# A residual add taken from VectorE and given to an accumulating transfer on GpSimd's queue

## The chip, the cores and the metric

The kernel runs on one core of one Trainium2 chip. The metric is the device time of one execution in microseconds (us). Five engines work in the core, each with its own queue of instructions taken in order: TensorE (PE in the profile, with its weight loads as PEld), VectorE (DVE), ScalarE (ACT), GpSimd (POOL) and SyncE (SP), which here only issues transfers. Engines and transfers wait for each other through semaphores.

## The reference

One block of a network over x of shape (1, 2048, 512), in float32. Two halves follow each other, each normalised, scaled and shifted, and each added to x through a gate (ga, gb) that comes from a small product of `silu(c)` with `w_mod`:

```python
h = _layernorm(x) * (1 + ca) + sa
x = x + ga * irfft2(rfft2(h) * (w_r + 1j * w_i))      # spectral half
h = _layernorm(x) * (1 + cb) + sb
act = mish(h @ w1 + b1)                               # 512 -> 1376
x = x + gb * (act @ w2)                               # 1376 -> 512
```

The change concerns only the last line: x plus gb times the output of the second product.

## The kernel before

x stays in the core as `x`, 128 partitions by 16 rows by 512 floats (`x[:, n, :]` for row group n). The first 170 us or so compute the spectral half; nothing in it is touched here.

The second half works on eight blocks b = 0 to 7 of 256 rows (two row groups each, n = 2b and 2b+1). The 1376 hidden features are cut into six tiles, so that there are `total = 48` steps s, six for each block; the queues are filled in the order in which the code is written (a manual schedule). A call `mlp(s)` does, in this order:

- `up(s)`: TensorE multiplies by w1 (L796, L798) into PSUM banks tagged A and D, two buffers each.
- `front(s)`: ScalarE adds the bias (L806) and VectorE adds a second PSUM half (L807); this frees the banks.
- `halves(s-1)`: ScalarE casts the activation to `ah` (L758), VectorE takes the rest as `al` (L759). TensorE uses each value as such a pair.
- `back(s)`: ScalarE's Mish (L813), and for most steps four small VectorE sums (L823).
- `down(s-2)`: TensorE multiplies by w2 (L849) into four banks of the block.

A block's sum is ready in the second step of the next block (i = 1). There `gather(b)` copies two banks out on ScalarE (L872, L873), and `chain(b)` adds them on VectorE (L878 to L886) into `rows`, which is `modr[:, 0:2]`, 128 x 1024 floats, one buffer for all blocks. One step later (i = 2) `residual(b)` finishes the sum (L891, L893), multiplies `rows` by the gate (L894), adds `rows` to the two row groups of `x` (L896), and SyncE stores these to the output (L898, 512 KB).

The last block differs. Its feature tiles come in another order, its step order is written so that most of its sum is gathered early: `gather(7)` and `chain(7)` stand in step 45, and `residual(7)` in step 46. Block 6 has its `chain` in step 43 and its `residual` in step 44, so `chain(7)`, which writes `rows` again, follows `residual(6)` by one step, where for the earlier blocks five steps lie between. For the rest of block 7 the gate is multiplied into w2 ahead of time (`gate_w2`, L778 on GpSimd, after loads by SyncE at L747), the plain tiles are split into pairs (`plain_w2`, L758 and L759), and `finish` runs the last products (`last_down`, L862 and L865) and adds them to `x` from PSUM (L938), with three small stores (L939).

Of the kernel before, what the change touches and what calls it, by code (L numbers as in the profile page):

```python
# [10 lines left out]
ALU = mybir.AluOpType  # L11
# [9 lines left out]
NB = 8  # L21
# [11 lines left out]
def tile_spectral_block(ctx: ExitStack, tc: tile.TileContext, x_d, w1_d, b1_d, w2_d,  # L33
                        c_d, xt_d, wm_d, wq_d, wz_d, kr_d, km_d, kc_d, ki_d, kf_d, kv_d, kw_d, kp_d, out_d):
    nc = tc.nc
# [831 lines left out]
    rows = modr[:, 0:2]  # L867
# [21 lines left out]
    def residual(b):  # L889
        p, q = done.pop(b)  # L890
        nc.vector.tensor_tensor(rows[:, 1, 256:], rows[:, 1, 256:], q[:, 0:256], op=ALU.add)  # L891
        if b < NB - 1:
            nc.vector.tensor_tensor(rows[:, 0, 256:], rows[:, 0, 256:], p[:, 256:], op=ALU.add)  # L893
        nc.vector.tensor_tensor(rows, rows, gbr.unsqueeze(1).to_broadcast([P, 2, D]), op=ALU.mult)  # L894
        xb = x[:, 2 * b:2 * b + 2, :]
        nc.vector.tensor_tensor(xb, xb, rows, op=ALU.add)  # L896
        if b < NB - 1:
            nc.sync.dma_start(ov[:, 2 * b:2 * b + 2, :], xb)  # L898

# [3 lines left out]
    def mlp(s, parts):  # L903
        b, i = divmod(s, NT)
        nxt = 2 * b + 2 if b < NB - 1 else None
        up(s)
        if i == 4 and nxt:
            for g in range(2):
                transpose_in(nxt, g)
        front(s)  # L910
        halves(s - 1, parts)
        parts = back(s)
        if i == 3 and nxt:
            norm_pair(nxt)
        if i == 4 and nxt:
            for g in range(2):
                split_in(nxt, g)
        down(s - LAG)
        if i == 1 and b:
            gather(b - 1)  # L920
            chain(b - 1)
        if i == 2 and b:
            residual(b - 1)
        if s == total - 3:
            gather(b)
            chain(b)
        if s == total - 2:
            residual(b)
        return parts
# [237 lines left out]
```

## Time and profile before

| What | Value |
|---|---|
| Median of 3 runs | 381.94 us (381.69 to 382.84) |
| Profiled execution, first to last instruction (span) | 380.1 us |
| Median less that span | 1.84 us |
| TensorE busy | 373.7 us (98%) |
| VectorE busy | 300.2 us (79%) |
| ScalarE busy | 250.5 us (66%) |
| GpSimd busy | 99.1 us (26%) |
| Granted TensorE clock | 1.000 |

For the profiled execution no time is given but its span; what lies around the span is taken as the 1.84 us between it and the median of the runs.

In the profile, L896 is line 896 of the kernel. A row of the timeline gives the start in us from the beginning of the span, the time in us that the merged instructions take together, engine, line, operation, what is written and read, the count, and in brackets how long the engine had been idle and what ended that. A row of a source line gives the smallest, median and largest duration in ns. The chain of waits is followed back from the last instruction of the kernel.

### The profile page before, as it was taken

The numbers are of one execution on the slowest core, as the hardware profiler recorded it, in microseconds if no ns is written. First come the engines' busy times: TensorE is split into PE (matmuls) and PEld (weight loads), VectorE is DVE, ScalarE is ACT, GpSimd is POOL, SyncE is SP. The second block draws the span as 40 slices with busy tenths as digits, with TensorE's granted clock in tenths as the row PEclk, the third lists the DMA queues.
The fourth block names the chain that finished last, engine by engine and source line by source line (L and its number), as shares of the span: only waits on it lengthen the run. The fifth ranks groups of instructions, "written<-read, shape, count | busy, mean of one in ns | idle before, by whom it ended". The sixth has DMA issues, their size and how long they took to land.

```text
span 380.1 us, 7142 instructions
## 1 busy us (share of the span) xinstructions
PE 373.7 (98%) x2612; PEld 340.0 (89%) x2612; DVE 300.2 (79%) x688; ACT 250.5 (66%) x532; POOL 99.1 (26%) x134
## 2 busy tenths in 40 slices
PE   8999999998999999999999999999999999999996
PEld 8999967778999989998998998998998999899985
DVE  2898968886989989989749758757865976887994
ACT  1798789995497558865844845845765674685751
POOL 0588747883664611300000000000000010017000
PEclk9999999999999999999999999999999999999999
DMA  7999997776454221111000100100100200222011
GB/s 235 380 354 344 362 359 237 252 231 212 128 140 143 77 85 58 56 30 55 3 0 2 55 2 0 58 0 3 55 2 0 78 0 2 75 67 82 2 55 55
DMA packets 21746, 41.14 MB, mean 108 GB/s; under 512 B 4016, under 2 KB 7184, under 8 KB 21456
## 3 DMA queue, kind: packets, MB, share of 16 engines
q1 hardware_dynamic: 19552, 33.75, 26.3%
q10 hardware_dynamic: 2160, 6.95, 6.2%
q8 instruction: 20, 0.33, 0.3%
q14 instruction: 14, 0.11, 0.1%
HBM read 36.49 MB, written 4.20 MB: 107 GB/s over the span
## 4 chain that ended last, share of the span: by engine, by line
PE 93%; DVE 3%; ACT 1%; DMA 1%; issue 0%; SPq 0%; ACTq 0%
PE bank L849 24%; PE bank L796 21%; PE bank L798 10%; PE bank L707 4%; PE bank L717 4%; PE bank L708 4%; PE bank L498 4%; PE bank L208 4%; PE bank L547 3%; PE bank L253 3%; PE bank L841 2%; PE bank L862 2%; PE bank L478 2%; PE bank L686 2%; PE bank L255 1%; PE bank L254 1%
## 5 line engine op out<-in xcount | busy, mean ns | idle before, releaser
L806 ACT ACTIVATE buf<-bank,b1n 128x256 f32<-128x256 f32 (+1 forms) x88 | 40.8, 471 | 66.8 <-PE bank L798 64.2
L807 DVE TENSOR_TENSOR buf<-buf,bank 128x256 f32<-128x256 f32 (+1 forms) x88 | 35.4, 417 | 37.3 <-ACT buf L806 37.2
L759 DVE TENSOR_TENSOR al<-buf,ah 128x512 fp32r<-128x512 f32 (+2 forms) x85 | 52.9, 645 | 0.9 <-ACT ah L758 0.9
L778 POOL TENSOR_TENSOR buf<-buf,modr 128x512 f32<-128x512 f32 (+1 forms) x3 | 4.0, 1322 | 182.8 <-DMA buf<-in_B_w_dram 175.6
L796 PE MATMUL bank<-h2e,w1h 128*128 128x512 f32 (+1 forms) x176 | 48.4, 397 | 0.0
L796 PE MATMUL bank<-h2o,w1h 128*128 128x512 f32 (+1 forms) x176 | 48.3, 396 | 0.0
L758 ACT CAST ah<-buf 128x512 fp32r<-128x512 f32 (+2 forms) x85 | 43.0, 548 | 1.4 <-DVE buf L823 1.1
L823 DVE TENSOR_TENSOR buf<-buf 128x128 f32<-128x128 f32 x148 | 40.8, 317 | 3.5 <-ACT buf L813 2.2
L813 ACT ACTIVATE buf<-buf 128x512 f32<-128x512 f32 (+1 forms) x48 | 28.6, 596 | 14.8 <-DVE buf L807 14.7
L849 PE MATMUL bank<-w2a,ah 128*128 128x256 f32 x161 | 34.9, 286 | 0.0
L796 PEld LDWEIGHTS bank<-h2e,w1h 128*128 128x128 f32 (+1 forms) x176 | 30.1, 187 | 4.5
L796 PEld LDWEIGHTS bank<-h2o,w1h 128*128 128x128 f32 (+1 forms) x176 | 30.1, 187 | 4.4
L849 PE MATMUL bank<-w2b,ah 128*128 128x256 f32 x147 | 31.8, 283 | 0.0
L798 PEld LDWEIGHTS bank<-h2o,w1l 128*128 128x128 f32 (+1 forms) x176 | 26.7, 185 | 4.2
L798 PEld LDWEIGHTS bank<-h2e,w1l 128*128 128x128 f32 (+1 forms) x176 | 26.7, 185 | 4.1
L798 PE MATMUL bank<-h2o,w1l 128*128 128x256 f32 (+1 forms) x176 | 27.8, 280 | 0.0
L798 PE MATMUL bank<-h2e,w1l 128*128 128x256 f32 (+1 forms) x176 | 27.8, 279 | 0.0
L849 PEld LDWEIGHTS bank<-w2a,ah 128*128 128x128 f32 x161 | 26.7, 191 | 0.0
L707 PE MATMUL bank<-kc,d 128*128 128x128 f32 x128 | 24.8, 276 | 0.5 <-ACT d L391 0.5
L708 PE MATMUL bank<-kc,d 128*128 128x128 f32 x128 | 24.7, 275 | 0.0
L849 PEld LDWEIGHTS bank<-w2b,ah 128*128 128x128 f32 x147 | 24.6, 191 | 0.0
L122 DVE BATCH_NORM_STATS2 st<-x 128x6 f32<-128x512 f32 x32 | 22.0, 689 | 0.4
(228 smaller groups left out, 981.1 us busy)
## 6 DMA issues: line engine op xcount, KB each, us to landing
buf<-in_B_w_dram SPq DMA_DIRECT2D x20, 256.0 KB, 3.0
x<-in_A_x_dram SPq DMA_DIRECT2D x16, 256.0 KB, 4.9
xring<-in_x_t_dram SPq DMA_DIRECT2D x16, 256.0 KB, 4.7
out_dram<-x SPq DMA_DIRECT2D x7, 512.0 KB, 2.6
buf<-in_w_mod_dram SPq DMA_DIRECT2D x9, 256.0 KB, 3.1
mraw<-in_km_dram SPq DMA_DIRECT2D x16, 128.0 KB, 4.7
wqa<-in_w_q_dram SPq DMA_DIRECT2D x4, 512.0 KB, 6.8
wqb<-in_w_q_dram SPq DMA_DIRECT2D x4, 512.0 KB, 7.2
```

Of the source, the lines that this page charges most:

```text
L122: nc.vector.bn_stats(t, x[:, n, :])
L707: nc.tensor.matmul(o, dj[:, 0:128], kc[0][:, n, :], start=True, stop=False)
L708: nc.tensor.matmul(o, dj[:, 64:192], kc[1][:, n, :], start=False, stop=True)
L758: nc.scalar.copy(h, r)
L759: nc.vector.tensor_tensor(l, r, plain(h), op=ALU.subtract)
L796: nc.tensor.matmul(ps, w1h[:, k, fs], h[:, k], start=(k == 0), stop=False)
L798: nc.tensor.matmul(ps[:, 0:256], w1l[:, k, fs], h[:, k, 0], start=False, stop=(k == 3))
L806: nc.scalar.activation(o, ps[:, 256:], AF.Identity, bias=b1n[:rows, f:f + 1])
L807: nc.vector.tensor_tensor(o, o, ps[:, 0:256], op=ALU.add)
L813: nc.scalar.activation(o, o, AF.Mish)
L823: nc.vector.tensor_tensor(o, p, q, op=op)
L849: nc.tensor.matmul(o, a[p][:, e], w2[t][q][:, r], start=(own and half == 0 and t == 1 and i == 0), stop=(end and i == 2 and (n, half) != ( ...
```

## The change

For blocks 0 to 6 the add L896 is no longer a VectorE instruction. GpSimd's queue issues a transfer from `rows` to the block's rows of `x` which adds what it carries to what lies there. Block 7 keeps its VectorE add.

```diff
         nc.vector.tensor_tensor(rows, rows, gbr.unsqueeze(1).to_broadcast([P, 2, D]), op=ALU.mult)
         xb = x[:, 2 * b:2 * b + 2, :]
-        nc.vector.tensor_tensor(xb, xb, rows, op=ALU.add)
+        if b < NB - 1:
+            nc.gpsimd.dma_start(xb, rows, accum_op=ALU.add)
+        else:
+            nc.vector.tensor_tensor(xb, xb, rows, op=ALU.add)
         if b < NB - 1:
             nc.sync.dma_start(ov[:, 2 * b:2 * b + 2, :], xb)
```

Which waits go with it, by the order of instructions in the two programs:

- each of the seven transfers waits, on GpSimd's queue, for L894;
- each of the seven stores (L898) waits, on SyncE's queue, for the transfer, where it waited for VectorE;
- the next block's L878, the first to write `rows` again, waits on VectorE's queue for the transfer (for blocks 1 to 7).

All other instructions stand where they stood.

## The prediction

> **What bounds the kernel now.** I read the page first (which engine is full), then the chain of waits, then the stretches of the second half, then the timeline of its last 25 us, where the changed code lies closest to the end.
>
> ```profile
> core 0: 380.1 us, clock 1.000
> ```
>
> ```profile
> PE 373.7 (98%) x2612; PEld 340.0 (89%) x2612; DVE 300.2 (79%) x688; ACT 250.5 (66%) x532; POOL 99.1 (26%) x134
> ...
> PE 93%; DVE 3%; ACT 1%; DMA 1%; issue 0%; SPq 0%; ACTq 0%
> ```
>
> The next rows are busy times (PE, PEld, DVE, ACT, POOL, then clock and transfers) in nine stretches of 22 us through the second half.
>
> ```profile
> 175.00:197.00 22.00, 22.00 (x158) 20.55 (x157) 14.93 (x34) 13.60 (x29) 0.00 (x0) 1.00 0.06 25
> ...
> 351.00:373.00 22.00, 22.00 (x147) 20.04 (x147) 20.69 (x40) 13.88 (x29) 0.00 (x0) 1.00 0.06 25
> sum 198.00, PE 198.00 PEld 182.81 DVE 150.31 ACT 123.01 POOL 9.74; mean PE 22.00 PEld 20.31 DVE 16.70 ACT 13.67 POOL 1.08
> ```
>
> TensorE is busy for 198.00 of 198.00 us, at full clock. Where the residuals run, nothing that VectorE does earlier can bring the end forward; VectorE can only make it later, by being late for TensorE. It is fullest in the last stretch (20.69 of 22).
>
> **The change part by part.** Removed: seven VectorE adds.
>
> ```profile
> L896 DVE TENSOR_TENSOR x<-x,modr x8: 1224/1224/1226, 176.9 to 370.4; 128x1024 f32<-128x1024 f32 x8
> ```
>
> That is 7 x 1.224 = 8.57 us of VectorE time, worth 0 at the end since TensorE has no gap for it to close. If TensorE did wait for VectorE somewhere unseen, the most it could bring is these 8.57 us; no row shows such a wait.
>
> Added: seven transfers of 512 KB inside the core, and the wait of the next L878 for each. Two pairs of rows show how much room the early blocks have, block 0 and block 5:
>
> ```profile
> 175.68 1.23 DVE L894 TENSOR_TENSOR modr<-modr 128x1024 f32<-128x1024 f32 x1
> ...
> 199.47 0.69 DVE L878 TENSOR_TENSOR modr<-bank,buf 128x512 f32<-128x512 f32 x1
> ```
>
> ```profile
> 327.12 1.23 DVE L894 TENSOR_TENSOR modr<-modr 128x1024 f32<-128x1024 f32 x1
> 328.38 1.22 DVE L896 TENSOR_TENSOR x<-x,modr 128x1024 f32<-128x1024 f32 x1
> ...
> 352.68 0.68 DVE L878 TENSOR_TENSOR modr<-bank,buf 128x512 f32<-128x512 f32 x1
> ```
>
> From the end of L894 to the next L878 there are 199.47 - 176.91 = 22.6 us and 352.68 - 328.35 = 24.3 us. Six of the seven waits are therefore covered by the four steps between; each would cost only what the transfer takes beyond 22 us. The seventh, block 6 before block 7, is not like them. VectorE's end game:
>
> ```profile
> 358.52 1.23 DVE L894 TENSOR_TENSOR modr<-modr 128x1024 f32<-128x1024 f32 x1
> 359.78 1.22 DVE L896 TENSOR_TENSOR x<-x,modr 128x1024 f32<-128x1024 f32 x1
> 360.92 1.28 DVE L759 TENSOR_TENSOR w<-raw,w 128x512 fp32r<-128x512 f32 x2
> 362.12 0.74 DVE L807 TENSOR_TENSOR buf<-buf,bank 128x256 f32<-128x256 f32 x2
> 362.79 0.69 DVE L759 TENSOR_TENSOR al<-buf,ah 128x512 fp32r<-128x512 f32 x1
> 364.04 0.69 DVE L878 TENSOR_TENSOR modr<-bank,buf 128x512 f32<-128x512 f32 x1 [0.57 <-ACT buf L872]
> ...
> 367.44 0.75 DVE L807 TENSOR_TENSOR buf<-buf,bank 128x256 f32<-128x256 f32 x2
> ...
> 371.89 0.68 DVE L759 TENSOR_TENSOR al<-buf,ah 128x512 fp32r<-128x512 f32 x1
> ```
>
> and TensorE beside it:
>
> ```profile
> 368.27 1.10 PE L796 MATMUL bank<-h2o,w1h 128*96 128x512 f32 x4
> ...
> 372.50 0.63 PE L862 MATMUL bank<-w2a,ah 128*128 128x512 f32 x2
> 372.97 0.39 PE L862 MATMUL bank<-w2a,al 128*128 128x512 f32 x1
> ```
>
> L894 of block 6 ends at 358.52 + 1.23 = 359.75. L878 of block 7 starts at 364.04, released by ScalarE's copy. So the transfer has 4.3 us before it starts to hold VectorE. From L878 to the `al` at 371.89 VectorE has no idle time, so a delay D of L878 moves all of it by D. Two uses follow. The products at 368.27 need an A bank that the first L807 of the pair at 367.44 has read: it ends half way through the pair, near 367.85, 0.4 before. The third product of the last w2 tile, 372.97, needs the `al` that ends at 372.57, again 0.4. Slack 0.4, taken as 0.35 for the semaphore; each further us of D is a us of the end, as everything after it is TensorE back to back. The point from which it costs is a transfer of 364.04 + 0.35 - 359.75 = 4.6 us, from the end of L894 to its landing.
>
> Queued behind the waiting L878 on VectorE are the rest of `chain(7)`, the split of a w2 tile, the L807 and `al` above; ScalarE's Mish waits for L807 and TensorE for both. Queued behind the transfer on GpSimd is nothing (below).
>
> How long does the transfer take? The trace has no transfer that adds, none within the core and none from GpSimd's queue. The nearest rows are plain stores of the same bytes:
>
> ```profile
> out_dram<-x SPq DMA_DIRECT2D x7, 512.0 KB, 2.6
> ...
> wqb<-in_w_q_dram SPq DMA_DIRECT2D x4, 512.0 KB, 7.2
> ...
> out_dram<-x SPq DMA_DIRECT2D x1, 256.0 KB, 2.0
> ```
>
> From the two stores: 256 KB more cost 0.6 us, so 512 KB is 1.2 us of data and 1.4 us fixed (estimate from these rows). Low end: it costs what the store costs, 2.6 us, and D is negative: no loss. Below that I exclude: it moves no fewer bytes. High end: the slowest 512 KB row, 7.2 us, on a full queue. Between them: an add touches the data three times (read the source, read the target, write), 3 x 1.2 = 3.6 us if the passes don't overlap, with the fixed 1.4 makes 5.0. GpSimd as the issuer: its shortest instructions over tiles of this kind take 1.3 us, where SyncE's issue takes 0.34, so 1.0 more.
>
> ```profile
> 333.49 1.30 POOL L778 TENSOR_TENSOR buf<-buf,modr 128x512 f32<-128x512 f32 x1 [27.43 <-DMA buf<-in_B_w_dram]
> 342.05 1.28 POOL L778 TENSOR_TENSOR buf<-buf,modr 128x512 f32<-128x512 f32 x1 [7.26 <-DVE buf L823]
> 343.29 5.82 POOL L778 TENSOR_TENSOR raw<-raw,modr 128x512 f32<-128x512 f32 x4
> ```
>
> ```profile
> 329.63 0.34 SPq L898 DMA_DIRECT2D out_dram<-x  x1
> 330.07 9.55 SPq L747 DMA_DIRECT2D buf<-in_B_w_dram  x2
> ```
>
> I take 6.0 us. It lies nearer the upper row than the lower since both what is unpriced (the add, the issuer) can only lengthen it. Landing at 359.75 + 6.0 = 365.75; loss 6.0 - 4.6 = 1.4 us.
>
> The DMA: Bandwidth & Descriptors page of the Trainium skill (section on the anatomy of a GpSimd transfer) fits about 2.0 us plus bytes over 436 GB/s: 3.2 us here as an estimate, for a plain copy. Collectives: The Full Stack, on why a reduce-scatter runs at half the rate of a gather, says that the add itself is free but two sources are read; another 1.2 us, so 4.4 us and no loss, 381.9 us in all. No row here shows either; the stores' 1.2 us of data agree with the rate.
>
> SyncE's queue: the store now waits for the landing, and loads stand behind it. Block 5: landing at 328.35 + 6.0 = 334.35, so the load that was issued at 330.07 goes 4.3 us later, and the multiply that stood at 333.49 stands near 337.8 to 339.1. GpSimd's next multiply waits until 342.05 for VectorE to free its buffer: 2.9 us remain, so this costs nothing below a transfer of 8.9 us, and then it first delays weights that are used 20 us later. Block 4's store has one load behind it, used later still. Block 6's has only the final stores:
>
> ```profile
> 361.03 0.34 SPq L898 DMA_DIRECT2D out_dram<-x  x1
> 375.50 2.21 SPq L939 DMA_DIRECT2D out_dram<-x  x2
> ```
>
> It would go at 365.8, ten us before them. GpSimd's queue: the transfer of block 6 stands behind the four multiplies, over at 343.29 + 5.82 = 349.11, ten us before L894 ends; that of block 5 issues at 328.35, before the multiply at 333.49. Cost 0.
>
> Sum, against the profiled execution: 380.1 + 0 (VectorE's 8.57) + 0 (six covered waits, the two queues) + 1.4 (the seventh wait) = 381.5 of span; with 1.84 around it 383.3, or 381.94 + 1.4 for the median: **383.3 us**, 0.37% slower.
>
> **The rivals.** No change that can be told (0.3%, 1.15 us, is about what a measurement of this kernel can tell): the transfer lands within 4.6 + 1.15 = 5.75 us. For it: the store's 2.6 us; with one read more, 3.8. Against: the store was issued by SyncE and adds nothing. It would give 381.9 to 383.1, most likely 381.9.
>
> Slower by more: the transfer is not started while VectorE works on two inputs from the same memory. The trace shows GpSimd and VectorE in each other's way: during the multiply at 333.49 one VectorE split takes far longer than its like.
>
> ```profile
> 330.18 1.16 DVE L759 TENSOR_TENSOR al<-buf,ah 128x384 fp32r<-128x384 f32 x2
> ...
> 333.78 1.43 DVE L759 TENSOR_TENSOR al<-buf,ah 128x384 fp32r<-128x384 f32 x1
> ```
>
> That is 1.43 against 0.6. If the transfer were held until the run of VectorE work after L894 is over (without L896: two splits, L807 x2, `al`, 1.28 + 0.74 + 0.69 = 2.7 us), it would land at 8.7 us and cost 4.1: 386.0. SBUF — State Buffer of the Trainium skill (section on who interferes with whom) warns that GpSimd cannot write a transfer's descriptors while VectorE is in a two-port mode, and says that an add of two tensors has no such mode; all work in this run is of that kind, so by that page the rival fails, and the trace shows no such transfer.
>
> Faster, the other sign: TensorE's records are modelled at their ends, and it might in truth lose a little to VectorE at every block. Then taking 1.224 us off VectorE seven times gives back some of 8.57 us; from 0.16 us a block (1.15 / 7) it would be told. At half of it, with a landing under 4.6 us: 377.7. Against it: 198.00 of 198.00 busy.
>
> **How the numbers follow.** Forecast (slower by a landing between 5.75 and about 8 us): 0.47. Held until VectorE is free, or a slower add: 0.10. No change: 0.38. Faster: 0.05. The range goes from 381.5, the fast landing within the runs' own spread, to 387.0, the held transfer and a us beyond; it leaves out the faster case and a transfer beyond 9.5 us. Faster 0.05, same 0.38, slower 0.57.
>
> **What would show it.** In the changed profile VectorE is idle before the last L878, released by a transfer, and L878 starts near 365.8; TensorE has its first gap of the second half before the products with 96 rows, about 1.4 us, and none earlier; the seven transfers have equal times from issue to landing, near 6 us. VectorE's busy time falls by 8.6 us. Wrong if L878 is again released by ScalarE (then no loss), if TensorE has gaps before 360 us, or if the median moves without a gap.

## The result: 383.13 us

The changed kernel takes 383.13 us (median of 20 runs, 381.93 to 383.71) against 382.01 us before (20 runs, 381.11 to 382.84): 1.1 us more, a ratio of 1.0026 with a 95% interval of 1.0017 to 1.0034, which is 0.65 to 1.30 us. The forecast was 383.3 us. The loss is real by its interval, though a little under the 0.3% that the prediction took for the least that can be told. The span of the profiled execution is 381.6 us (380.1 before).

The page of the changed kernel, its engines and its new rows (line engine operation count, busy time and mean ns; in the last row the KB of each transfer and the median us from issue to landing):

```profile
PE 374.8 (98%) x2612; PEld 340.8 (89%) x2612; DVE 290.7 (76%) x681; ACT 251.1 (66%) x532; POOL 105.0 (28%) x141
...
L897 POOL DMA_DIRECT2D x<-modr x7 | 6.2, 890 | 168.4 <-DVE buf L807 128.7
...
x<-modr POOLq DMA_DIRECT2D x7, 512.0 KB, 4.6
```

VectorE's busy time fell by 9.5 us (8.6 had been forecast), and TensorE's rose by 1.1. The waits of TensorE show the one new row; the other five, all before 140 us, stand in both kernels:

```profile
PE bank L796 <- DVE buf L807: 0.5, 1, 0.5
```

The timeline of VectorE at the end of the changed kernel, and of GpSimd and TensorE beside it:

```profile
359.53 1.23 DVE L894 TENSOR_TENSOR modr<-modr 128x1024 f32<-128x1024 f32 x1
360.68 1.29 DVE L759 TENSOR_TENSOR w<-raw,w 128x512 fp32r<-128x512 f32 x2
361.88 0.74 DVE L807 TENSOR_TENSOR buf<-buf,bank 128x256 f32<-128x256 f32 x2
362.55 0.68 DVE L759 TENSOR_TENSOR al<-buf,ah 128x512 fp32r<-128x512 f32 x1
365.74 0.69 DVE L878 TENSOR_TENSOR modr<-bank,buf 128x512 f32<-128x512 f32 x1 [2.51 <-ACT buf L806]
```

```profile
361.06 0.88 POOL L897 DMA_DIRECT2D x<-modr  x1 [10.83 <-DVE modr L894]
```

```profile
363.32 1.09 PE L796 MATMUL bank<-h2o,w1h 128*128 128x512 f32 x4
...
369.61 1.16 PE L796 MATMUL bank<-h2o,w1h 128*96 128x512 f32 x4 [0.52 <-DVE buf L807]
```

The gate multiply L894 ends at 360.76, GpSimd takes up the transfer 0.30 later, and VectorE stands idle for 2.51 us before L878. The row names ScalarE's L806, which is not what L878 reads; the chain of waits names the transfer, with its landing at 361.06 + 4.56 = 365.62:

```profile
361.06 4.56 DMA x<-modr
...
365.74 0.69 DVE modr L878
```

The whole execution lies later by some 0.66 us than the one before already at 157 us, ahead of the first changed instruction, so absolute times of the two are not to be compared (in the traces below, with transfers and without, the same offset lies between -0.65 and +0.66 us). A measure free of that is the time from the start of step 46's products to the start of those with 96 rows (step 47): 368.27 - 362.66 = 5.61 us before, 369.61 - 363.32 = 6.29 after. That is a stall of 0.68, and the rest up to the last add of VectorE is 0.12 longer (8.78 against 8.66). By these two profiles, one of each kernel, the change costs 0.8 us.

### The profile page after: what moved, and what is told of

The parts are those of the page before. It is cut to its first block, busy times and chain, and to the rows that moved or that the text cites. A ratio compares the mean times of both kernels' runs of the same rounds, so it can differ in the third digit from the quotient of the medians.

```text
span 381.6 us, 7151 instructions
## 1 busy us (share of the span) xinstructions
PE 374.8 (98%) x2612; PEld 340.8 (89%) x2612; DVE 290.7 (76%) x681; ACT 251.1 (66%) x532; POOL 105.0 (28%) x141
## 4 chain that ended last, share of the span: by engine, by line
PE 71%; DVE 11%; ACT 7%; issue 5%; DMA 3%; POOL 2%; ACTq 1%; SPq 0%; DVEq 0%; POOLq 0%
PE bank L849 20%; PE bank L796 17%; PE bank L798 9%; PE bank L208 4%; PE bank L253 3%; PE bank L841 2%; DVE st L122 2%; PE bank L707 2%; PE bank L708 2%; PE bank L717 2%; DVE x L720 2%; DVE w2a L759 2%; POOL raw L778 2%; PE bank L862 1%; PE bank L264 1%
## 5 line engine op out<-in xcount | busy, mean ns | idle before, releaser
L806 ACT ACTIVATE buf<-bank,b1n 128x256 f32<-128x256 f32 (+1 forms) x88 | 41.0, 472 | 73.7 <-PE bank L798 71.0
L807 DVE TENSOR_TENSOR buf<-buf,bank 128x256 f32<-128x256 f32 (+1 forms) x88 | 35.3, 416 | 44.7 <-ACT buf L806 44.7
L759 DVE TENSOR_TENSOR al<-buf,ah 128x512 fp32r<-128x512 f32 (+2 forms) x85 | 52.4, 639 | 0.7 <-ACT ah L758 0.7
L897 POOL DMA_DIRECT2D x<-modr x7 | 6.2, 890 | 168.4 <-DVE buf L807 128.7
L796 PE MATMUL bank<-h2o,w1h 128*128 128x512 f32 (+1 forms) x176 | 48.4, 396 | 0.5 <-DVE buf L807 0.5
L796 PE MATMUL bank<-h2e,w1h 128*128 128x512 f32 (+1 forms) x176 | 48.4, 397 | 0.0
L823 DVE TENSOR_TENSOR buf<-buf 128x128 f32<-128x128 f32 x148 | 39.9, 311 | 3.5 <-ACT buf L813 2.2
L796 PEld LDWEIGHTS bank<-h2o,w1h 128*128 128x128 f32 (+1 forms) x176 | 30.1, 187 | 5.1 <-DVE buf L807 0.7
L796 PEld LDWEIGHTS bank<-h2e,w1h 128*128 128x128 f32 (+1 forms) x176 | 30.1, 187 | 4.5
```

The lines of the kernel that those rows point to most:

```text
L759: nc.vector.tensor_tensor(l, r, plain(h), op=ALU.subtract)
L796: nc.tensor.matmul(ps, w1h[:, k, fs], h[:, k], start=(k == 0), stop=False)
L806: nc.scalar.activation(o, ps[:, 256:], AF.Identity, bias=b1n[:rows, f:f + 1])
L807: nc.vector.tensor_tensor(o, o, ps[:, 0:256], op=ALU.add)
L823: nc.vector.tensor_tensor(o, p, q, op=op)
```

## The experiments

Theory W is the prediction's: only the wait of block 7's first write to the shared `rows` costs. Its rivals: F, a transfer from GpSimd's queue has a price of its own, wherever it stands; Q, the loads of w2 that now stand behind later stores on SyncE's queue. Medians in one group share their runs of the kernel before.

**Six transfers without the seventh.**

```diff
-        if b < NB - 1:
+        if b < NB - 2:
             nc.gpsimd.dma_start(xb, rows, accum_op=ALU.add)
```

> Blocks 0 to 5 by the adding transfer, block 6 by VectorE again. Theory W (only the wait of block 7's first write to the shared rows costs): six covered transfers cost nothing, 382.0 us, ratio 1.000 within 0.001, no gap of TensorE before the products with 96 rows. Rival F (a transfer from GpSimd's queue has a price of its own, fixed or spread over the blocks, of some 0.1 us a block): 0.6 us or more remain, ratio at least 1.0015. Rival Q (SyncE's queue: the loads of w2 behind the later stores): the whole loss remains, 383.1 us, as the delayed loads stand behind the stores of blocks 4 and 5.

382.36 us against 382.18 before, ratio 1.0008 (0.9993 to 1.0023). In the trace no wait of TensorE after 140 us, and 5.61 us between the two starts, as before:

```profile
363.14 1.09 PE L796 MATMUL bank<-h2o,w1h 128*128 128x512 f32 x4
...
368.75 1.16 PE L796 MATMUL bank<-h2o,w1h 128*96 128x512 f32 x4
```

The times alone leave a price of up to 0.9 us open, which takes in F's 0.6 and comes close to Q's 1.1. It is the trace, in which TensorE waits for nothing, that speaks against both; F is tested again below.

**The seventh alone.**

```diff
-        if b < NB - 1:
+        if b == NB - 2:
             nc.gpsimd.dma_start(xb, rows, accum_op=ALU.add)
```

> Only block 6 by the adding transfer, blocks 0 to 5 by VectorE. Theory W: the whole loss with one transfer, 0.8 us by the profile's gap (0.7 us before the products with 96 rows and 0.1 at the last split) to 1.1 us by the medians, so 382.8 to 383.1 us, ratio 1.002 to 1.003; last L878 near 5.0 us after the end of the gate multiply. Rival F: a seventh of the loss if spread, 382.2 us; Rival Q: nothing, 382.0 us.

382.77 us against the same 382.18, ratio 1.0015 (1.0005 to 1.0024). Here VectorE's idle time is put down to the transfer itself, and the stall is back, 6.16 us between the starts, 0.55 more than before:

```profile
365.21 0.69 DVE L878 TENSOR_TENSOR modr<-bank,buf 128x512 f32<-128x512 f32 x1 [2.66 <-DMA x<-modr]
```

```profile
362.91 1.09 PE L796 MATMUL bank<-h2o,w1h 128*128 128x512 f32 x4
...
369.07 1.16 PE L796 MATMUL bank<-h2o,w1h 128*96 128x512 f32 x4 [0.40 <-DVE buf L807]
```

One transfer of the seven makes most of the stall. By the medians the loss is 0.59 us, less than the 0.8 to 1.1 that W expected, though the interval (0.19 to 0.92) reaches into it; it leaves out F's seventh and Q's nothing.

**All seven, with another buffer for block 7.** Nothing is left out; block 7's sum goes to `raw`, whose contents are used up.

```diff
-    rows = modr[:, 0:2]
+    def sums(b):
+        return st["raw"][:, 0:2] if b == NB - 1 else modr[:, 0:2]
...
         p, q = done[b]
+        rows = sums(b)
...
         p, q = done.pop(b)
+        rows = sums(b)
...
             raw = pm.tile([P, 4, D], F32, name="raw", tag="h2e")
+            st["raw"] = raw
```

> All seven transfers, but block 7 gathers its sum in another buffer (the first half of raw, read for the last time in step 43), so that nothing of block 7 waits for block 6's transfer. Theory W: the loss is gone, 382.0 us, ratio 1.000 within 0.001, and the last L878 is released by ScalarE. Rival F: 0.6 us or more remain with the same seven transfers. Rival Q: 383.1 us.

382.26 us against 382.18, ratio 1.0001 (0.9990 to 1.0012). The seven transfers are there; the wait is not, and L880, which is the L878 of this kernel, follows ScalarE again:

```profile
360.90 0.88 POOL L900 DMA_DIRECT2D x<-modr  x1 [10.82 <-DVE modr L897]
```

```profile
363.64 0.69 DVE L880 TENSOR_TENSOR raw<-bank,buf 128x512 f32<-128x512 f32 x1 [0.57 <-ACT buf L873]
```

This is the same amount of transfer with the dependence gone, and the loss is gone with it.

**The add left out.**

```diff
-        if b < NB - 1:
-            nc.gpsimd.dma_start(xb, rows, accum_op=ALU.add)
-        else:
+        if b == NB - 1:
             nc.vector.tensor_tensor(xb, xb, rows, op=ALU.add)
```

> The add of blocks 0 to 6 is left out altogether, by VectorE and by transfer (their output is x without the gated rows); stores wait for nothing new. All theories that take TensorE as the bound: VectorE's 8.57 us are worth nothing, 382.0 us, ratio 1.000 within 0.001. If VectorE's time did tell somewhere unseen: faster, up to 373.4 us; from 380.9 us it would be told.

384.2 us, ratio 1.0062 (1.0040 to 1.0085): slower with less work, which no theory had expected. The edit did more than it was meant to. With nothing writing x, six stores no longer had anything to wait for and went ahead, five from 159 us and the sixth at 164, and with them two of the loads of w2 that stand behind them on SyncE's queue. First the kernel before, then this one (SyncE's stores; ScalarE's issue of the gate's spread, L52):

```profile
164.38 0.33 ACTq L52 DMA_DIRECT2D modr<-gb  x1
```

```profile
159.09 3.90 SPq L899 DMA_DIRECT2D out_dram<-x  x5
...
168.87 0.33 ACTq L52 DMA_DIRECT2D modr<-gb  x1
169.30 0.84 ACT L806 ACTIVATE buf<-bank,b1n 128x256 f32<-128x256 f32 x2 [3.60 <-PE bank L849]
```

```profile
PE bank L841 <- DVE modr L878: 0.7, 1, 0.7
PE bank L841 <- DVE modr L886: 0.6, 1, 0.6
```

L52 waits on ScalarE's own queue for the small transfer of the gate before it (L48, 2 KB). With the stores in flight that transfer took 6.2 us to land where it had taken 2.1, so L52 went 4.1 us later after L48's issue; L806 stood behind it, VectorE's L878 came late, and TensorE waited 1.3 us. From the L796 before these waits to the next one it is 4.61 us in place of 2.79, which is 1.8 of the 2.0 us by the medians. So much the trace shows; that the early transfers held the small one up was tested with the next kernel.

**A sliver of the add.** VectorE adds two columns of each row group in blocks 0 to 6, so that the stores keep their places; the other columns are left out.

```diff
-            nc.gpsimd.dma_start(xb, rows, accum_op=ALU.add)
+            nc.vector.tensor_tensor(xb[:, :, 0:2], xb[:, :, 0:2], rows[:, :, 0:2], op=ALU.add)
```

> As the kernel before, but in blocks 0 to 6 VectorE adds only the first two columns of each row group (the rest of the gated rows is left out), so that each store still waits for its block and goes at its old place. If the loss with the add left out came from the six stores that went early, and not from VectorE's missing time, it is gone here; TensorE as the bound says 382.1 us, ratio 1.000 within 0.001, no gap of TensorE after 140 us. If VectorE's 8.4 us tell somewhere: 380.9 us or less. If VectorE's missing work by itself is harmful: near 384 us again.

381.88 us against 382.22 before, ratio 0.9994 (0.9982 to 1.0006), with no wait of TensorE after 140 us. VectorE's adds fell from 1.22 to 0.17 us each, 7.4 us in all, and the end did not move (the interval leaves a gain of at most 0.7 us). The gate's small transfer lands after 2.4 us again. The loss with the add left out came with the freed stores and the loads that followed them; which of the two weighs more is not shown.

**Copies in place of the add.** From GpSimd's queue, then from SyncE's; in blocks 0 to 6 the gated rows replace x.

```diff
-            nc.gpsimd.dma_start(xb, rows, accum_op=ALU.add)
+            nc.gpsimd.dma_start(xb, rows)
```

> The transfer from GpSimd's queue copies instead of adding (in blocks 0 to 6 the gated rows replace x). It shares issuer, bytes written and place, and reads one side instead of two. If the prediction's terms are right (1.4 fixed, 1.2 us for each pass over the data, 1.0 for the issuer, with the measured total of 4.6 from issue to landing in place of its 6.0), the copy lands 1.2 to 2.4 us earlier, 2.2 to 3.4 us from issue, and the loss is gone: 382.0 us. Rival: the add itself is free and the time is all issuer and landing: 4.6 us as before, 383.1 us.

```diff
-            nc.gpsimd.dma_start(xb, rows, accum_op=ALU.add)
+            nc.sync.dma_start(xb, rows)
```

> The same copy from SyncE's queue (in blocks 0 to 6 the gated rows replace x). By the prediction's terms it is a store of 512 KB with another target: 2.6 us from issue to landing, 1.0 less than the copy from GpSimd's queue; 382.0 us. Rival: a transfer within the core is dearer than one to the output whoever issues it: 3.5 us or more.

382.5 us (ratio 1.0007, 0.9995 to 1.0019) and 382.44 us (1.0006, 0.9996 to 1.0017) against 382.09: no loss that can be told, and no stall in either trace. With GpSimd's copy the profile still names the transfer as what released the last L878, but that is 0.40 us after the start of step 46's products, where it had been 1.38 in the kernel before: the wait is there and costs nothing. What they were made for is the time from issue to landing, from GpSimd and from SyncE:

```profile
x<-modr POOLq DMA_DIRECT2D x7, 512.0 KB, 3.2
```

```profile
x<-modr SPq DMA_DIRECT2D x7, 512.0 KB, 3.0
```

So of the 4.6 us, the add makes 1.4, the issuer 0.2, and a target within the core instead of the output 0.4 (the store takes 2.6). SyncE's copy had been expected at the store's 2.6. GpSimd's own part of the issue took 0.86 us for the add and 0.53 for the copy, so up to 0.3 of the 1.4 may lie there rather than in the second read; no run parts the two.

**Half of each block by transfer.**

```diff
-            nc.gpsimd.dma_start(xb, rows, accum_op=ALU.add)
+            nc.vector.tensor_tensor(xb[:, 0], xb[:, 0], rows[:, 0], op=ALU.add)
+            nc.gpsimd.dma_start(xb[:, 1], rows[:, 1], accum_op=ALU.add)
```

> In blocks 0 to 6 VectorE adds the first row group and the transfer the second, half the bytes. If the time of a transfer goes with its bytes beside a fixed part (1.2 us for each pass over 512 KB): 1.2 to 1.8 us less from issue to landing, near 3.1 us, but issued as early, so the last L878 is released by ScalarE or about then, and the loss is gone: 382.0 us. Rival: mostly fixed: above 4 us, and at least 0.3 us of the loss remains.

381.99 us against 382.09, ratio 0.9996 (0.9987 to 1.0005): the loss is gone. 256 KB land 3.3 us after the issue, 1.3 less than 512 KB, and L878 follows ScalarE:

```profile
x<-modr POOLq DMA_DIRECT2D x7, 256.0 KB, 3.3
```

```profile
362.88 0.69 DVE L878 TENSOR_TENSOR modr<-bank,buf 128x512 f32<-128x512 f32 x1 [0.57 <-ACT buf L872]
```

**Block 6 twice.** Its gated rows are added twice.

```diff
             nc.gpsimd.dma_start(xb, rows, accum_op=ALU.add)
+            if b == NB - 2:
+                nc.gpsimd.dma_start(xb, rows, accum_op=ALU.add)
```

> Block 6's rows are added twice, the second transfer waiting for the first (block 6's output has the gated rows twice). Theory W, with its one us of end for each us of wait: the second landing is 4.9 us after the first, so L878 starts near 10 us after the gate multiply and the end comes 4.9 us later than with one: 388.0 us. Rival: the end has more slack than the 0.4 us read from the trace, or part of the wait is absorbed (half of it: 385.6 us).

389.44 us (median of 4 runs) against 382.09, ratio 1.0195 (1.0169 to 1.0221), 7.35 us and more than W's 5.9. The wait is as W says: L878 starts at 369.81, 5.77 us later than before when both are counted from the start of step 46's products (362.66 in both), and TensorE stalls 11.02 - 5.61 = 5.41 us, 0.36 less, which is the slack read before. The rest is the clock. The timeline of TensorE, and its stretches (busy times of the five engines, then the granted clock):

```profile
373.68 2.02 PE L796 MATMUL bank<-h2o,w1h 128*96 128x512 f32 x4 [5.24 <-DVE buf L807]
```

```profile
365.00:370.00 5.00, 3.44 (x23) 2.98 (x21) 0.18 (x1) 0.98 (x2) 0.86 (x1) 1.00 0.55 105
370.00:375.00 5.00, 1.32 (x3) 0.95 (x4) 4.90 (x12) 0.63 (x1) 0.00 (x0) 0.81 0.26 105
375.00:380.00 5.00, 5.00 (x28) 4.41 (x27) 3.48 (x5) 1.80 (x4) 0.00 (x0) 0.84 0.00 0
```

Taken us by us, the granted clock was 0.50 from 374 to 376 and 1.00 again from 377. After the pause the four products take 2.02 us where they took 1.10, and from there to the first of the last adds it is 7.86 us in place of 6.52: another 1.3 us. 5.4 + 1.3 makes the 6.8 by which the span is longer.

**Twenty-eight small transfers.** Block 7 with its own buffer, as above, and each add cut in four.

```diff
-            nc.gpsimd.dma_start(xb, rows, accum_op=ALU.add)
+            for i in range(2):
+                for c in (slice(0, 256), slice(256, D)):
+                    nc.gpsimd.dma_start(xb[:, i, c], rows[:, i, c], accum_op=ALU.add)
```

> Block 7 with its own buffer, and each of the seven adding transfers cut in four, 28 of 128 KB in place of 7. Theory W: nothing waits for them, 382.1 to 382.4 us, ratio 1.000 within 0.001. Rival F, a price spread over the transfers (the whole 1.1 us over seven is 0.16 us each): 28 of them cost 4.5 us, 386.6 us; if the 0.3 us that the six transfers may have cost were real and went with their number, 1.4 us, 383.5 us.

382.27 us against 382.22, ratio 1.0003 (0.9994 to 1.0012). Four times as many transfers cost nothing where nobody waits: F's 4.5 us and its 1.4 both lie outside the interval. F falls.

## Why the prediction was right

The mechanism was right: one wait, at the place that was named. That the time came out so near, 383.13 for 383.3, is in part luck. The forecast was given for a landing between 5.75 and about 8 us after L894; it came after 4.86, which is the condition under which the prediction expected no change that can be told, 381.9 to 383.1. The transfer was priced 1.1 us too long and the queues' share was put at nothing, and the two errors partly cancel: 0.35 of the 0.68 us of stall came by the queues. L878's start at 365.74, forecast as 365.8, agrees only by the 0.66 us by which the whole execution lies later.

- **VectorE's 8.57 us are worth 0**: right, shown by the sliver for 7.4 of them.
- **Six waits are covered, the seventh is not**: right. Without the seventh there is no stall, alone it makes 0.55 us of one, and with another buffer for block 7 the other six and the seventh cost nothing together.
- **Slack and slope**: the slack of 0.35 us came out as 0.36 with the doubled transfer, and every further us of wait was a us of stall. The place where TensorE would wait first, the products with 96 rows behind L807, is the one.
- **The time of the transfer, 6.0 us**: too long, the term that was mis-sized. From the end of L894 to the landing it took 0.30 + 4.56 = 4.86 us. The two extra passes were put at 2.4 us and the add cost 1.4; the issuer was put at 1.0, after a GpSimd multiply that has little in common with an issue, and cost 0.2; the target within the core, put at 0, cost 0.4, and the start after L894 0.3. The prediction's other estimate, by Collectives: The Full Stack in the Trainium skill (section on why a reduce-scatter runs at half the rate), one source more to read, 1.2 us, is nearer to the add's 1.4. The anatomy formula of DMA: Bandwidth & Descriptors in the Trainium skill, 3.2 us, is what the copy from GpSimd's queue took. The two together gave 4.4 us and no loss; what they missed is 0.2 us of the add and the 0.3 ahead of the issue.
- **The queues cost 0**: not quite. The multiply of block 5's weights, delayed as worked out, to 337.86, fell on a VectorE instruction that had been alone:

```profile
337.86 1.29 POOL L778 TENSOR_TENSOR buf<-buf,modr 128x512 f32<-128x512 f32 x1 [7.43 <-DMA buf<-in_B_w_dram]
```

```profile
338.62 1.09 DVE L699 TENSOR_TENSOR h2o<-buf,h2o 128x512 fp32r<-128x512 f32 x1 [0.88 <-ACT h2o L698]
...
345.96 3.12 DVE L759 TENSOR_TENSOR al<-buf,ah 128x384 fp32r<-128x384 f32 x2
```

  L699 took 1.09 where it takes 0.69, the buffer for the next load came free later, and with it the four multiplies beside which L759 took 3.12 in place of 2.66. Counted from step 46's products, L894 ends 0.35 us later than before (2.56 us ahead of them instead of 2.91). The four traces in which the multiply falls on this L699 show it: there the next load goes 0.4 to 0.5 us later and L894 ends 2.55 to 2.66 us ahead (2.57 without the seventh). In the six others, where the multiply stays or is moved to another place, the load is on time to within 0.01 us and L894 ends 2.82 (the seventh alone) or 2.91 ahead, in both copies, the halves and the quarters too. That the buffer is the link is read from these rows; no run was made to take it away by itself. Without a wait for a transfer it costs 0.1 us at most; with the wait it adds to it.
- **The sum**: the wait moved L878 by 0.69 us through the transfer (4.98 us from L894 to L878, 4.29 before) and by 0.35 through the later L894; less the slack of 0.36 that is the stall of 0.68, and 0.8 us at the end. The same sum for the seventh alone, 0.83 (5.12 us from L894 to L878) + 0.09 - 0.36 = 0.56, agrees with the 0.55 read there. The 1.4 of the forecast is nearly twice that and the medians' 1.1 lies between. What the medians have beyond the profile, 0.3 us, is within their interval and stays open. The seven transfers were not alike, though the prediction had expected equal times: block 0's took 5.2 us to land, block 4's 6.2, the others 4.5 to 4.8. These are the same blocks in each trace that has the seven or six whole transfers, and the seventh, where it carries the whole add, takes 4.5 to 4.7 in each, so a slow seventh is no likely cause of the rest.
- **The held transfer**: the rival fell. The seventh, beside VectorE's work on two inputs, took 4.56 us, the median of all seven is 4.6.

## What to carry to other kernels

VectorE, off the path, was relieved of 7.4 us of work and the end did not move; the dependence that comes with such a relief is then what is left: look where the buffer is written again soonest, not at the average block. A transfer is priced from the end of what it waits for to the start of what waits for it, and here an add within the core took 1.4 times as long as a copy. A load that is pushed back on a queue should be followed to the engine on which its user then falls, here 0.35 us of the wait. When a wait on a shared buffer is the loss, another buffer whose contents are used up removes it; and when an experiment leaves out a write, look what was waiting for it, since it will run early.

## What the runs showed of the hardware

- A pause of TensorE of 0.5 us did not touch its clock (1.00 throughout). After one of 5.24 us the clock was 0.50 from 374 to 376 us and back at 1.00 from 377, which cost 1.3 us on top of the pause. TensorE: Matmul & The Clock Gate of the Trainium skill (part 1, the clock gate) says that an idle window of about 3.4 us takes the clock to half; the 0.50 and the products after the pause, 2.02 us for 1.10, agree.
- Adding transfers within the core landed 3.3 us after their issue for 256 KB and 4.6 for 512 KB: 2.0 us fixed and 1.3 for each 256 KB, an estimate worked out from these two. A copy of 512 KB from the same queue took 3.2.
- While six stores of 512 KB and the loads behind them went out on SyncE's queue, a 2 KB transfer on ScalarE's queue took 6.2 us to land instead of 2.1, and the one that waited for it went 4.1 us later.
- A VectorE instruction on two inputs of 128 x 512 floats (L699) took 1.09 us beside a GpSimd multiply, and 0.69 us alone.
